# The block sums of the first MLP weight on GpSimd instead of VectorE, with new instruction orders on every engine

## The chip, the cores and the metric

The kernel runs on one core of a Trainium2 chip. The metric is the device time of one execution in microseconds; the median of a few runs is the number that counts, lower is better.

## What is computed

Four batches of 576 tokens with 512 features (8 heads of 64) go through three stages. The first is an attention with two parts that are added: a dense one on queries, keys and values pooled by 4, and a local one in which every token sees the tokens less than 4 away.

```python
out_d = sm_attn(q_d, k_d, v_d)               # q_d: mean of 4 neighbours
out_up = np.repeat(out_d, factor, axis=2)
scores = np.where(np.abs(pos[:, None] - pos[None, :]) < factor, scale * q @ k.T, -1e9)
x = out_up + softmax(scores) @ v             # heads side by side: 512 features
```

The second mixes by a two-dimensional Fourier transform, normalises and applies an MLP; the third is a gated convolution.

```python
u = x + np.real(np.fft.fft(np.fft.fft(x, axis=1), axis=2))
un = (u - mean) / np.sqrt(var + 1e-06)
x = u + np.maximum(un @ w_ch1, 0.0) @ w_ch2  # 512 -> 2048 -> 512
gate = sigmoid(conv of 5 taps along the tokens)
out = (gate * (x @ w_val)) @ w_out
```

## The kernel before

Work is cut into 12 units of 192 tokens, three to a batch. A unit runs its LayerNorm, the MLP and the gated convolution; the attention and the Fourier mixing of the next batch run in between. TensorE multiplies float16 numbers: each float32 operand is split into a high and a low half and three products of halves are added. The splitting, the softmax, the LayerNorm and all sums fall to VectorE, ScalarE and GpSimd, the loads and stores to the DMA queue of SyncE. The first unit (function `steps32`, L1276 and L1287) still multiplies in float32, since the split weights are not ready then.

**Startup.** Batch 0 has a startup of its own (`chain0`): the scores of the local attention come in three groups g0, g1, g2 (matmuls `dS`, L1608 and L1618), VectorE takes their maxima (`score_max`, L1631, tile `dmx`), ScalarE the exponentials, VectorE divides (`score_norm`), the Fourier mixing follows (`pp`, `DS`, additions into `X` at L521), then the mean of a token (`mean`, matmuls `st` at L1888) and its subtraction (`centre`, L1892, result `u`). The first matmul of the MLP (`ph<-u,W`, L1276) waits for `u`. All weights are rounded in the same time by integer steps on VectorE (L614 and L515, tiles `W`). The attention of batch 1 starts here too: its queries and keys are loaded into tiles called `X` (L524, `X<-in_k_dram`, in two halves) and its scores are `dS<-X` at L822.

**Seven products.** Units 6 to 11 compute the first MLP matmul (`seven`, L1333) with seven block products in place of eight. That needs sums and differences of blocks of the first weight. They are made once, in units 3 and 4, by eight calls of `sums_w1` (S_SUMS = 3.4 to 4.3): a call loads four blocks of 128x256 from a copy of the rounded weight in DRAM (`w1f`, written by `store_w1`, L1235, as soon as each eighth of the weight is rounded), makes four sums (L1243, tile `sx`), splits them (`so`) and stores them to DRAM (`sums`, L1248); `load_sums` brings them back for every unit (L524, `W<-sums`).

```python
for o, p, q, op in ((2, 1, 2, ALU.add), (1, 0, 1, ALU.subtract), (0, 2, 0, ALU.subtract), (3, 3, 0, ALU.subtract)):
    V.tensor_tensor(out=x[:, o], in0=x[:, p], in1=x[:, q], op=op)          # L1243
```

**Order.** What each engine does in which order is written out by hand: the table `ORDER` (L53) holds for every engine, the DMA queue among them, a list of event numbers (`118` or `118.2`, the third instruction of event 118), and at the end of the program every instruction is chained to the one before it in its list. An instruction that waits therefore holds up all that stand behind it on its engine, a store in SyncE's list holds up the loads behind it.

Of the kernel before, what the change touches and what calls it, by code (L numbers as in the profile page):

```python
# [54 lines left out]
0 2 1 3 4 11 5 13 7 6 14 8 9 15.0 16.0 10 15.4 12 16.1 15.2 15.1 15.3 195.1 201 119.2 122.1 15.5 123.1 16.2 119.0  # L55
195.0 123.0 205 185.0 119.3 119.1 122.0 204 206 170 199 172.1 203 200 171 173 172.0 174 185.2 219.1 185.1 318.0 202
237.1 219.0 237.0 238 292 317.1 316.1 293 296.0 270.0-1 296.1 270.2 297 317.0 316.0 279 332 367.1 367.0 349 318.1-2
353 378.1 368.0 378.2 368.1 378.0 369 370.0 435.1 370.1 387.1 387.0 378.4 378.3 387.2 394.1 394.0 387.3-4 394.2
397.0-1 386 488.0 394.3 397.2 394.4 398 402.0-1 488.1 402.2 397.4 397.3 435.0 436.0 437.0 418 436.1 409.1 409.0 402.3
409.2 402.4 415.1 409.4 415.0 409.3 415.2 422.0-2 415.4 415.3 475 437.1 422.4 422.3 494.1 494.0 437.2 491 462 492.0  # L60
505 492.1 493 520 530 540 503 528.1 528.0 551 528.2 562.0 544 583.1 562.1 569 583.0 548 576.1 576.0 581 563 591 598
605 613 621.1 621.0 628 635.1 635.0 611 643.1 643.0 622 651 657 665 672 679.1 641 679.0 670 680 684 703 706 707
""",
    "gpsimd": """
0.0 5 136.1 136.0 137 0.1 139 183.0 294.0 195.0-1 183.1-3 193 219.1 219.0 219.2 237.1 195.2 225.0-2 237.0 237.2 225.3
238.1 238.0 238.2 267.1 267.0 275 277 121 282.1 280.1 280.0 282.0 283.1 283.0 285.0 294.1-3 291.0-1 298.0 291.2-5
# [6 lines left out]
30.1 30.0 20 21 18 0 32.0-1 32.3 32.2 25 28 41.1 41.0 48.0 131.0 38 23 48.1 27 48.2 56 48.3 54.0 31 131.1 54.1-3 65.0  # L73
58.0 34 65.1 42 63 59 71.0-1 71.3 71.2 77.1 77.0 58.1 73 86 81.0 55 85 60 68 130 83 75 52.0 81.1 52.1-3 81.2 92 70.0
# [6 lines left out]
302.1 224.4 249.4 249.1 302.0 253.5 249.2 241 269 274 253.6 257.0 236 246 257.3 225.0 303.0 292.0 253.7 249.5 253.8
304.0 302.3 253.9 243 278 253.10-11 257.1-2 303.3 261.0 292.1 267.1 253.12-13 284 257.4-5 263.0 292.3-4 292.2 253.14
306.0 263.1 263.3 299.0 263.2 251 288 293.0 292.5 303.1 261.1 302.2 293.1 263.4 300 263.5 407.0 303.2 261.2-3 293.2
304.2 304.1 267.0 293.3 305 295.1 261.4-5 295.0 293.4-5 271.0-2 299.1 273.0 299.2-3 273.2 273.1 296.0 310 271.3 273.3
275.1 314 327 275.0 277.0-1 304.3 275.2 277.2 296.1-3 335 280.0 296.4 280.1 296.5 306.2 306.1 282 297.0 283 297.1
297.3 309 299.4 407.1 306.3 261.6 297.4 285.0-2 323 297.5 297.2 407.2 285.3 286 291.0-1 342 291.2 338 326.0 291.3
294.0 291.4 326.1 294.1-2 350.0 322 313.0 350.1 291.5 339 326.2 311.0 291.6 326.3 298.2 298.1 354 311.1 333.1 357 364
313.1 328.3 328.2 333.0 329.3 298.0 328.1 332 331.3 328.0 334.3 329.1 329.0 329.2 331.0-1 407.4 319 331.2 334.0 334.2
334.1 371 341 347.0 344.0 379 344.1 333.2 355.0 347.1 345.1 462.1 324 345.0 347.2 366 333.3 347.3-5 355.1-2 356.1 388
347.6 355.3 356.2 407.3 347.7-9 356.0 359.0-1 345.2-3 361.0-1 395 400 347.10 359.2 356.3 378.0 376.3 378.1-2 406.0  # L90
# [387 lines left out]
def attn_moe_kernel(ctx, tc, q_t, k_t, v_p, v_w, w1, w2, w_val, conv_t, w_out, c_feat, c_seq, c_band, c_eye, c_plm, out):  # L478
# [23 lines left out]
    V, A, G, T = nc.vector, nc.scalar, nc.gpsimd, nc.tensor  # L502
# [734 lines left out]
    def sums_w1(i, kc):  # L1237
# [4 lines left out]
        for o, p, q, op in ((2, 1, 2, ALU.add), (1, 0, 1, ALU.subtract), (0, 2, 0, ALU.subtract), (3, 3, 0, ALU.subtract)):  # L1242
            V.tensor_tensor(out=x[:, o], in0=x[:, p], in1=x[:, q], op=op)  # L1243
# [871 lines left out]
```

## Time and profile before

| what | us |
|---|---|
| runs | 656.77, 656.94, 660.54; median 656.94 |
| profiled execution | 658.47 |
| span in its trace | 656.7 |
| TensorE busy | 643.9 (98%) |
| VectorE busy | 526.3 (80%) |
| ScalarE busy | 353.9 (54%) |
| GpSimd busy | 105.6 (16%) |

The trace covers the span from the first instruction to the last; 1.8 us of the profiled execution lie around it. Engines are called PE (TensorE), PEld (its weight loads), DVE (VectorE), ACT (ScalarE), POOL (GpSimd) and SPq (the DMA queue of SyncE). A granted clock of 1.00 is TensorE's upper level of 2.4 GHz, 0.50 the lower of 1.2 GHz. "[1.67 <-DMA X]" at the end of a row means that the engine stood idle for 1.67 us before it and that the DMA of X ended the wait.

### The profile page before, as it was taken

The numbers are of one execution on the slowest core, as the hardware profiler recorded it, in microseconds if no ns is written. First come the engines' busy times: TensorE is split into PE (matmuls) and PEld (weight loads), VectorE is DVE, ScalarE is ACT, GpSimd is POOL, SyncE is SP. The second block draws the span as 40 slices with busy tenths as digits, with TensorE's granted clock in tenths as the row PEclk, the third lists the DMA queues.
The fourth block names the chain that finished last, engine by engine and source line by source line (L and its number), as shares of the span: only waits on it lengthen the run. The fifth ranks groups of instructions, "written<-read, shape, count | busy, mean of one in ns | idle before, by whom it ended". The sixth has DMA issues, their size and how long they took to land.

```text
span 656.7 us, 20454 instructions
## 1 busy us (share of the span) xinstructions
PE 643.9 (98%) x8646; PEld 576.8 (88%) x8647; DVE 526.3 (80%) x1148; ACT 353.9 (54%) x1051; POOL 105.6 (16%) x162
## 2 busy tenths in 40 slices
PE   9999899999999999999999999999999999999997
PEld 4777799999998887998988898997899989998995
DVE  3999799889898868779989958996878768686644
ACT  2886558788445656687453788644232333324222
POOL 0000131310121713510310163032100200200000
PEclk9969899999999999999999999999999999999999
DMA  9949485104442012334273372253445134232401
GB/s 318 411 167 312 165 320 172 60 2 141 145 140 91 1 36 75 103 119 145 75 249 115 103 259 84 84 183 118 133 135 170 66 130 138 90 130 87 157 2 49
DMA packets 44303, 89.99 MB, mean 137 GB/s; under 512 B 3391, under 2 KB 24895, under 8 KB 43186
## 3 DMA queue, kind: packets, MB, share of 16 engines
q1 hardware_dynamic: 44210, 88.67, 39.8%
q8 instruction: 68, 1.11, 0.7%
q14 instruction: 25, 0.20, 0.1%
HBM read 73.77 MB, written 16.65 MB: 138 GB/s over the span
## 4 chain that ended last, share of the span: by engine, by line
PE 77%; DVE 5%; DMA 4%; POOL 2%; ACT 2%; SPq 1%; issue 1%; DVEq 0%; ACTq 0%; POOLq 0%
PE pc L1382 23%; PE ph L1312 11%; PE ph L1333 7%; PE val L1487 6%; PE out L1503 6%; PE p L1333 5%; PE ph L1276 3%; PE pc L1287 3%; DMA X<-in_k_dram 2%; PE ab L1063 1%; PE dS L822 1%; PE st L1147 1%; PE pp L1086 1%; DMA out_dram<-osb 1%; PE pq L1086 1%; PE po L995 1%
## 5 line engine op out<-in xcount | busy, mean ns | idle before, releaser
L1382 PE MATMUL pc<-hh,W 128*128 128x192 f16 x1232 | 169.2, 246 | 0.0
L1382 PEld LDWEIGHTS <-W 128*128 128x128 f16 x1848 | 152.7, 98 | 3.5 <-issue 1.2
L1382 PE MATMUL pc<-hl,W 128*128 128x192 f16 x616 | 130.1, 246 | 0.0
L1312 PE MATMUL ph<-u,W 128*128 128x192 f16 x960 | 93.9, 246 | 0.0
L1312 PEld LDWEIGHTS <-W 128*128 128x128 f16 x960 | 79.8, 98 | 4.6 <-issue 2.0
L1333 PEld LDWEIGHTS <-W 128*128 128x128 f16 x1632 | 78.7, 98 | 3.0 <-issue 1.2
L515 DVE SCALAR_TENSOR_TENSOR W<-X,cw,W 128x192 f32<-128x192 f32 x160 | 63.0, 430 | 4.8 <-ACT W L1450 4.5
L1333 PE MATMUL ph<-u,W 128*128 128x96 f16 x960 | 65.0, 206 | 0.5 <-ACT r L1350 0.3
L1487 PE MATMUL val<-yy,W 128*128 128x192 f16 x576 | 58.5, 246 | 1.5 <-DVE yy L515 1.5
L1345 ACT ACTIVATE hh<-r 128x384 f16<-128x384 f32 x48 | 23.8, 518 | 64.8 <-DVE r L521 53.5
L1487 PEld LDWEIGHTS <-W 128*128 128x128 f16 x576 | 47.4, 98 | 3.4 <-issue 2.1
L1333 PE MATMUL p<-u,W 128*128 128x96 f16 x672 | 48.2, 206 | 0.1
L1503 PE MATMUL out<-W,gh 128*128 128x512 f16 x144 | 46.2, 379 | 0.0
L521 DVE TENSOR_TENSOR r<-ph,r 128x384 f32<-128x384 f32 (+1 forms) x48 | 21.9, 456 | 24.8 <-PE ph L1333 20.5
L836 ACT ACTIVATE dP<-dS,dmx 128x64 f32<-128x64 f32 x120 | 36.0, 335 | 0.4
L521 DVE TENSOR_TENSOR r<-p,r 128x192 f32<-128x192 f32 (+1 forms) x72 | 28.1, 419 | 6.3 <-PE p L1333 4.3
L1316 ACT ACTIVATE hh<-ph 128x384 f16<-128x384 f32 x40 | 19.0, 484 | 22.1 <-PE ph L1312 14.7
L515 DVE SCALAR_TENSOR_TENSOR hl<-r,hh 128x384 f16<-128x384 f32 x48 | 25.7, 554 | 5.7 <-ACT hh L1345 5.2
L515 DVE SCALAR_TENSOR_TENSOR W<-W,W 128x1024 int32<-128x1024 int32 x24 | 29.7, 1248 | 0.1
L515 DVE SCALAR_TENSOR_TENSOR hl<-ph,hh 128x384 f16<-128x384 f32 x40 | 21.7, 551 | 7.2 <-ACT hh L1316 7.0
L1503 PE MATMUL out<-W,gl 128*128 128x512 f16 x72 | 27.3, 380 | 0.1
L836 ACT ACTIVATION_READ_ACCUMULATOR dP<-dS,dmx 128x1 f32 x120 | 27.4, 229 | 0.0
(306 smaller groups left out, 1423.3 us busy)
## 6 DMA issues: line engine op xcount, KB each, us to landing
W<-sums SPq DMA_DIRECT2D x32, 512.0 KB
W<-in_moe_w_ch_dram SPq DMA_DIRECT2D x12, 1024.0 KB
sm<-sums SPq DMA_DIRECT2D x16, 512.0 KB
out_dram<-osb SPq DMA_DIRECT2D x17, 256.0 KB
vw<-in_vw_dram SPq DMA_DIRECT2D x8, 512.0 KB
w1f<-W SPq DMA_DIRECT2D x8, 512.0 KB
sums<-so SPq DMA_DIRECT2D x16, 256.0 KB
v<-in_vp_dram SPq DMA_DIRECT2D x24, 144.0 KB
```

Of the source, the lines that this page charges most:

```text
L515: return eng.scalar_tensor_tensor(out=out, in0=in0, scalar=scalar, in1=in1, op0=op0, op1=op1)
L521: return eng.tensor_tensor(out=out, in0=a, in1=b, op=ALU.add)
L836: A.activation(out=s_[:, z, a], in_=pss[par][:, z, a], func=AF.Exp, scale=SCALE, bias=mx[:, par, z, a:a + 1], accum_out=su[:, par, z, a:a ...
L1276: T.matmul(out=ps[:, e], lhsT=W[AT[kc * 2 + m // 8] + 1][:, o:o + 128], rhs=u()[:, kc, :], start=(kc == 0), stop=(kc == 3))
L1287: T.matmul(out=c["ps"][m // 2][:, m % 2], lhsT=W[9 + g][:, o:o + 128], rhs=hs[g // 2][:, g % 2, e, :], start=(kk == 0 and m % 2 == 0), sto ...
L1312: T.matmul(out=ps[:, e], lhsT=w1_ap(pw, kc, 2 * g + e), rhs=uh[px][:, kc, :], start=(t == 0), stop=(t == 11))
L1316: A.activation(out=h_, in_=ps, func=AF.Relu)
L1333: T.matmul(out=out[:, e * HT:e * HT + HT], lhsT=w(pw, kc, e), rhs=b_[x](px, kc), start=(kc, pw, px) == (0, 0, 0), stop=(kc, pw, px) == (1, ...
L1345: A.activation(out=h[0], in_=x, func=AF.Relu)
L1382: T.matmul(out=ps[m // 2][:, m % 2], lhsT=w2_ap(pw, kk, m), rhs=x[px][:, e], start=(kk == 0 and (pw, px) == (0, 0) and m % 2 == 0), stop=( ...
L1487: T.matmul(out=ps[:, e], lhsT=wv_ap(pw, kc, 2 * mh + e), rhs=m_["y"][px][:, kc, :], start=(t == 0), stop=(t == 11))
L1503: T.matmul(out=ps, lhsT=(gh, gl)[px][:, kc, t * 128:(t + 1) * 128], rhs=wo_ap(pw, kc), start=(n == 0), stop=(n == 11))
```

## The change

One line of the program changes the engine of the 32 sums, and the table of orders is replaced for all five engines. It is 7 lines longer, so that a line number below 53 stays and every later one grows by 7 (L1243 becomes L1250, L524 becomes L531).

```diff
-            V.tensor_tensor(out=x[:, o], in0=x[:, p], in1=x[:, q], op=op)
+            G.tensor_tensor(out=x[:, o], in0=x[:, p], in1=x[:, q], op=op)
...
     "sync": """
-0 2 1 3 4 11 5 13 7 6 14 8 9 15.0 16.0 10 15.4 12 16.1 15.2 15.1 15.3 195.1 201 119.2 122.1 15.5 123.1 16.2 119.0
...
+0 2 1 3 4 5.1 11 13 16.0 7 5.0 6 14 8 9 12 10 15.0 15.4 15.3 15.2 15.1 16.2 16.1 195.1 203 119.3 15.5 122.0 199 123.0
```

Apart from the 32 sums each engine has the instructions that it had, in another order.

First, VectorE at the start of the program. The tiles dmx_222 are the maxima of score group g0 (dS_181 and dS_183), dmx_293 those of g1. Before:

```order
L1631 TENSOR_REDUCE dmx_293<-dS_250 128x8
L1631 TENSOR_REDUCE dmx_293<-dS_248 128x8
L1631 TENSOR_REDUCE dmx_222<-dS_181 128x4
L1631 TENSOR_REDUCE dmx_222<-dS_183 128x4
L1689 TENSOR_REDUCE qkT_136<-X_134 128x288
L1689 TENSOR_REDUCE qkT_136<-kTa_137 128x288
L537 MEMSET ones_105 128x128
L1646 TENSOR_SCALAR dsu_233<-dsu_233 128x8
L1647 RECIPROCAL dsu_233<-dsu_233 128x8
```

Now:

```order
L1638 TENSOR_REDUCE dmx_222<-dS_181 128x4
L1638 TENSOR_REDUCE dmx_222<-dS_183 128x4
L1638 TENSOR_REDUCE dmx_293<-dS_248 128x8
L1638 TENSOR_REDUCE dmx_293<-dS_250 128x8
L1696 TENSOR_REDUCE qkT_136<-X_134 128x288
L1696 TENSOR_REDUCE qkT_136<-kTa_137 128x288
L1653 TENSOR_SCALAR dsu_233<-dsu_233 128x8
L1654 RECIPROCAL dsu_233<-dsu_233 128x8
L525 TENSOR_TENSOR dP_235<-dP_235,dsu_233 128x256
```

The maxima of g0 moved ahead of those of g1, and the memset behind the first division.

Second, the DMA queue of SyncE where the keys of batch 1 are loaded. `w1f<-W_114` and `w1f<-W_115` are stores of rounded eighths of the first weight, `X<-in_k_dram` the two halves of the keys. Before, eight rows behind the store `w1f<-W_114`:

```order
L524 DMA X<-in_k_dram 128x2x582
L1235 DMA w1f<-W_115 128x1024
L524 DMA vw<-in_vw_dram 128x512
L524 DMA raw<-in_moe_w_ch_dram 128x1024
L524 DMA W_123<-in_moe_w_ch_dram 128x2x1024
L524 DMA X<-in_k_dram 128x2x582
```

Now:

```order
L531 DMA v_1223<-in_vp_dram 72x2x256
L1242 DMA w1f<-W_115 128x1024
L531 DMA raw<-in_moe_w_ch_dram 128x1024
L531 DMA W_121<-in_moe_w_ch_dram 128x2048
L531 DMA X<-in_k_dram 128x2x582
L1242 DMA w1f<-W_114 128x1024
L531 DMA X<-in_k_dram 128x2x582
L531 DMA W_122<-in_moe_w_ch_dram 128x2x1024
L531 DMA X<-in_q_dram 128x2x576 x2
L1242 DMA w1f<-W_116 128x1024
```

The first half of the keys stood behind the store of W_114 and the second behind that of W_115 too; now the first half stands behind the store of W_115, which comes first, and the second right behind the store of W_114.

Third, GpSimd in the midst of units 3 and 4, where the sums now stand (ptv and vr pool the values of a batch, sx_4222, sx_4360, sx_4426 are those of three calls; sq_4526 belongs to the LayerNorm of a unit). Before:

```order
L521 TENSOR_TENSOR ptv_3881<-v4_3877 72x256
L521 TENSOR_TENSOR vr_3856<-v4_3878 72x256
L521 TENSOR_TENSOR vr_3856<-vr_3856,ptv_3881 72x256
L521 TENSOR_TENSOR sq_4526<-sq_4526 128x384
L521 TENSOR_TENSOR sq_4526<-sq_4526 128x192
L1037 TENSOR_TENSOR fs_4590<-X_2960 128x577
L1037 TENSOR_TENSOR fs_4643<-X_2960 128x577
```

Now:

```order
L528 TENSOR_TENSOR ptv_3881<-v4_3877 72x256
L528 TENSOR_TENSOR vr_3856<-v4_3878 72x256
L528 TENSOR_TENSOR vr_3856<-vr_3856,ptv_3881 72x256
L1250 TENSOR_TENSOR sx_4222<-sx_4222 128x256 x4
L1250 TENSOR_TENSOR sx_4360<-sx_4360 128x256 x4
L1250 TENSOR_TENSOR sx_4426<-sx_4426 128x256 x3
L528 TENSOR_TENSOR sq_4526<-sq_4526 128x384
L1250 TENSOR_TENSOR sx_4426<-sx_4426 128x256
L528 TENSOR_TENSOR sq_4526<-sq_4526 128x192
L1044 TENSOR_TENSOR fs_4590<-X_2960 128x577
```

Eleven sums, 128x256 each, moved in ahead of the squares of the LayerNorm, and one between them.

## Rows read from the trace of the kernel before

**Rows 1.** The page, part 1: busy time, share of the span, instructions.
```profile
PE 643.9 (98%) x8646; PEld 576.8 (88%) x8647; DVE 526.3 (80%) x1148; ACT 353.9 (54%) x1051; POOL 105.6 (16%) x162
```

**Rows 2.** Windows of 41 us: length, busy PE, PEld, DVE, ACT, POOL, PEclk, DMA share, GB/s.
```profile
41.00:82.00 41.00, 37.14 (x428) 31.38 (x428) 37.31 (x74) 25.61 (x74) 2.98 (x14) 0.90 0.75 255
82.00:123.00 41.00, 41.00 (x422) 39.93 (x421) 38.65 (x53) 28.85 (x92) 9.92 (x13) 1.00 0.60 211
```

**Rows 3.** Waits of PE over the whole span: us in total, times, longest.
```profile
PE dS L822 <- DMA X<-in_k_dram: 1.7, 1, 1.7
PE val L1487 <- DVE yy L515: 1.5, 1, 1.5
```

**Rows 4.** Windows of 10 us, columns as in rows 2.
```profile
60.00:70.00 10.00, 10.00 (x85) 7.28 (x83) 9.61 (x20) 8.67 (x22) 0.77 (x9) 1.00 0.99 337
70.00:80.00 10.00, 8.24 (x67) 7.22 (x65) 7.49 (x13) 3.63 (x11) 2.21 (x6) 0.83 0.20 76
```

**Rows 5.** Timeline of DVE from 10 us on: start, length, instruction, idle before.
```profile
10.15 1.95 DVE L1631 TENSOR_REDUCE dmx<-dS 128x8 f32<-128x512 f32 x4 [10.15 <-PE dS L1618]
...
19.28 1.29 DVE L1631 TENSOR_REDUCE dmx<-dS 128x8 f32<-128x512 f32 x2 [0.69 <-PE dS L1618]
```

**Rows 6.** Timeline of PE from 4 and from 12 us.
```profile
8.94 1.40 PE L1618 MATMUL dS<-kTa,X 64*58 64x64 f32 x80
...
12.23 3.46 PE L1753 MATMUL po<-vw,plm 64*72 64x256 f32 x15
...
18.12 1.10 PE L1618 MATMUL dS<-kTa,X 64*58 64x64 f32 x62
```

**Rows 7.** DVE by line and shape, 10 to 12.1 us: busy, mean ns.
```profile
L1631 DVE TENSOR_REDUCE dmx<-dS 128x4 f32<-128x256 f32 x2 | 0.7, 416 | 0.0
```

**Rows 8.** Timeline of PE at the end of the startup.
```profile
69.12 0.90 PE L1888 MATMUL st<-X,ones 128*128 128x192 f32 x4
...
72.16 0.29 PE L822 MATMUL dS<-X 64*58 64x64 f32 x2 [1.67 <-DMA X<-in_k_dram]
72.37 1.36 PE L1888 MATMUL st<-X,ones 128*128 128x192 f32 x4
...
74.78 3.52 PE L1276 MATMUL ph<-u,W 128*128 128x192 f32 x16
```

**Rows 9.** Timeline of DVE at the same place.
```profile
70.45 0.81 DVE L521 TENSOR_TENSOR X<-mir,DS 128x289 f32<-128x289 f32 x2
73.77 0.95 DVE L1892 TENSOR_TENSOR u<-X,st 128x768 f32<-128x768 f32 x1 [2.51 <-PE st L1888]
```

**Rows 10.** Window of 1 us on PE: busy, PEclk, DMA share, GB/s.
```profile
73.00:74.00 1.00, 1.00 (x14) 0.50 0.06 25
```

**Rows 11.** The chain that ended last, 80 to 90 us.
```profile
83.60 2.60 PE ph L1276 x16
```

**Rows 12.** Timeline of SyncE's DMA queue, 17 to 64 us (length is the issue).
```profile
41.44 0.36 SPq L1235 DMA_DIRECT2D w1f<-W  x1
...
59.44 0.34 SPq L1235 DMA_DIRECT2D w1f<-W  x1
...
61.65 0.47 SPq L524 DMA_DIRECT2D X<-in_k_dram  x1
```

**Rows 13.** The line of the sums: ns min/median/max, first and last start.
```profile
L1243 DVE TENSOR_TENSOR sx<-sx x32: 406/424/832, 271.5 to 371.2; 128x256 f32<-128x256 f32 x32
```

**Rows 14.** POOL by line and shape: busy, mean ns, idle before.
```profile
L518 POOL TENSOR_TENSOR dP<-dP,dsu 128x256 f32<-128x256 f32 x4 | 3.3, 830 | 20.0 <-ACT osb L1521 16.4 <-DVE dsu L840 3.6
```

**Rows 15.** Timeline of SyncE's queue, 363 to 378 us.
```profile
376.54 1.64 SPq L524 DMA_DIRECT2D W<-sums  x2
```

**Rows 16.** Timeline of PE, 384 to 387 us: the first product from a sum is in this row.
```profile
385.95 0.29 PE L1333 MATMUL ph<-u,W 128*128 128x96 f16 x3
```

**Rows 17.** Timeline of POOL, 211 to 220 us: two equal products.
```profile
215.15 1.50 POOL L518 TENSOR_TENSOR r<-r,vv 128x192 f32<-128x192 f32 x1
...
218.59 0.59 POOL L518 TENSOR_TENSOR r<-r,vv 128x192 f32<-128x192 f32 x1
```

More of the change, by code (lines that the diff above doesn't have):

```diff
@@ L70 @@
+419.0 423 424 402 427.1 427.0 409 415.0-2 444.0 415.3 444.1 422 430.1 450 430.0 488.1 488.0 488.2 499.0 491.0 467
+491.1 499.1 492 491.2 499.2-3 493.1 493.0 493.2 433 546.0-1 535 539 546.2-3 545.1 545.0 550 553.1 553.0 554 559 609
 639
@@ L81 @@
[L81 to L90, printed above, removed]
@@ new lines @@
+546.13 546.11-12 570.0-2 570.5 546.14 570.6 570.3-4 546.15 594.0-1 574 594.2 590 578.0-2 578.5 578.3 578.6 578.4
+594.3-4 579.2 579.1 579.3 582.1 594.5 584.1 585.0-3 585.5 594.6 585.4 585.6 579.0 594.7-8 582.2 582.0 582.3 584.3
+584.0 584.2 593.0-1 586.1 593.2-3 593.5 594.9 586.3 586.2 586.0 594.10 593.4 593.6 634.3 594.11-15 594.17 592.0
+599.0-1 594.16 599.2-3 599.5 599.4 599.6 670.1 594.19 594.18 592.1 609.0 603 596.0 609.1 620 596.1 607.0-2 607.5 607.3
+607.6 607.4 609.2 608.1-2 608.0 615.0-2 615.5 608.3 612.2 615.6 615.3-4 612.3 612.1 612.0 609.3-6 624.0-3 624.5
@@ new lines @@
+96.7 96.10 96.16 96.11 96.14-15 96.17-18 96.20 96.19 96.21-22 96.24 96.23 96.25 96.28 96.26 96.29 96.27 96.30-31 99
+100 101.0 101.2-3 101.1 101.4-6 101.8-9 101.12 101.7 101.13 101.16-17 101.20-21 101.24-25 101.28-29 101.10-11
+101.14-15 101.18-19 101.22-23 101.26-27 101.30-31 126.0 128.2 128.0-1 128.3 111.6 111.12 111.0 111.13-14 111.1 111.7
+111.15-16 111.2-3 111.17 111.4-5 111.8-11 115.24 115.0-1 115.12 115.25-26 115.2-6 115.27 115.7-10 115.28 115.11
+115.13-15 115.29-30 115.16 115.31-32 115.17 115.33 115.18 115.34-35 115.19-23 120.0 120.12-16 120.6 120.1-3 120.17
@@ new lines @@
+571.1 571.8 571.2 571.9-10 571.3-5 571.11-12 571.18 571.13-14 571.19-20 571.15-17 571.21-23 578.0-11 572.0 572.6
+572.1-2 572.7-8 572.3-4 572.9 572.5 572.12-14 572.10-11 572.15 572.18-19 572.16 572.20-23 572.17 573.0-4 573.6 573.5
+573.12 573.7 573.13 573.8-10 573.14 573.11 573.15-23 594.0 578.48 578.12 578.72 578.13-16 578.49-51 578.73 578.17
+578.52 578.18 578.74 578.19-29 578.53-57 578.30-37 578.75 578.38-47 578.58-65 578.76 578.66-68 592.0-5 578.69
+578.77-78 578.70-71 578.79-83 592.6-21 585.0-6 585.48 585.7 585.24-25 585.8-11 585.49 580.6 580.0-3 580.7-9 580.4-5
@@ new lines @@
+627.2 627.8 627.3 629.49 629.12-15 629.50 629.28-29 629.16-19 629.51-53 629.30-31 629.54-57 629.72 629.58-59 629.73
+629.20 629.60 629.21-22 629.32-33 629.23 629.34 629.61-65 629.35 629.74-75 629.66-69 629.76-78 629.36 629.70-71
+623.0-1 629.37-47 629.79-80 627.4-5 627.12 627.9-10 627.13-15 629.81-83 627.11 627.18-20 627.16 627.21-23 627.17
+623.2-19 630.0 630.6 630.1-2 637.0-1 626.22-23 637.2-3 623.20-23 630.7-8 630.3 630.9-11 630.4-5 630.18-20 630.12-13
+630.21-22 630.14-16 630.23 630.17 637.4-6 637.24 637.7 637.25-26 637.8-11 631.0 631.6-8 631.1-2 631.9-10 631.3-5
@@ new lines @@
+631.12-15 631.11 631.16-23 639.0 637.12 637.27 637.72 637.48 637.13-14 637.49-50 637.15 637.28 637.73 637.29 637.16-17
+637.30-41 637.18 637.42-47 637.51-53 637.74 637.54-59 637.75-76 637.60 637.77-80 637.61-63 637.19 637.64 637.20-21
+637.81-83 637.22-23 637.65-71 632.0-1 632.6 632.2 632.7 632.3-5 632.8-10 632.12 632.11 632.18-22 632.13 632.23
+632.14-17 641.0-8 645.0-2 645.24 645.3-4 645.25 645.5 645.26 645.6-10 645.27-28 645.11 641.9-11 645.12 645.72
+645.13-15 639.1 645.16 645.73 645.48 645.29-32 645.49 645.33-34 645.74 645.50 645.35-38 645.51 645.39 645.17-18
@@ new lines @@
+653.51-53 653.20 653.25 653.21 653.26-33 653.54 653.34-35 653.55-56 653.36 653.57 653.37-38 653.58 653.39-40 653.74-75
+653.59 653.22-23 653.60-61 653.41-43 653.62-63 653.76-79 653.64-65 653.44-47 653.66-68 653.80 652.12-17 653.69-70
+653.81-83 653.71 649.11 649.0 649.18-20 649.1 649.21-22 649.2-5 649.12-15 658.24 658.0-2 658.25 652.18 649.16-17
+649.23 654.0-1 654.6 654.2-3 658.3-5 658.26 658.6-9 658.72 658.10 658.48 658.11 658.73-74 654.4 654.7-11 654.5
+654.12-13 654.18 654.14 654.19 654.15 654.20-23 654.16-17 655.19-23 652.19-23 658.75 658.12 658.49 658.27 658.13
@@ L357 @@
+688.0 688.12 688.1-7 688.13 688.8-11 688.14-23 703 701 704 705 707.0 706.0-6 707.1-6 706.7-11 707.7-11
 """,
```

540 lines of the change are left out of this document (261 added, 279 removed), and 8 rows, old and new, of the table ORDER.

## The prediction

> **What bounds the kernel now.** I read the page first. TensorE is busy for 643.9 us of a span of 656.7, VectorE for 526.3 and GpSimd for 105.6 [rows 1]: TensorE sets the time, and what can be won are the 12.8 us in which it is idle and the stretches in which it runs at its lower clock. The windows of 41 us say where these lie. Between 41 and 82 TensorE is busy for 37.14 of 41 us at a mean clock of 0.90, and from 82 to 123 for all of its 41 us at 1.00 [rows 2]. So the loss is in the startup and next to nothing in the stretch behind it. The list of TensorE's waits names the largest single one: scores of batch 1 that wait 1.7 us for a DMA of keys; next comes one of 1.5 us for VectorE in `val` [rows 3]. In the last startup window before the loss VectorE is busy for 9.61 of 10 us, and in the next, from 70 to 80, for 7.49 [rows 4]: up to about 71 us VectorE has no holes to speak of and paces the start, and behind that TensorE does. The timeline of VectorE shows where it does wait: its first instruction comes at 10.15, when the scores are there, and at 19.28 it waits 0.69 for the scores of group g2 [rows 5].
>
> **The sums themselves.** 32 instructions of 0.424 (the median) leave VectorE: 13.6 us between 271.5 and 371.2 [rows 13]. They join GpSimd. The trace shows no sum of this shape there; the nearest row is a product of the same shape, 128x256 with two operands, at 830 ns mean [rows 14], so I take 32 x 0.83 = 26.6 us, on an engine that is busy 16% of the span. TensorE, busy 98% of the span [rows 1], is the bound there, so the 13.6 us come off an engine that is not, and I count them at 0. They could be worth at most what small waits there are; the cost on the other side is the second rival's.
>
> **The start of VectorE.** Before, the four maxima wait for the scores of g1, start at 10.15 and take 1.95 [rows 5]. Now the two maxima of g0 come first, and TensorE's order has the last nine products of g0 ahead of the 32 of g1, where before g1's stood first. The 40 products take from 8.94 to 10.34, 0.035 each [rows 6]; nine are done at 8.94 + 0.32 = 9.26, and with the delay of rows 5 (32 products end at 10.06, VectorE starts at 10.15, so 0.09) the maxima of g0 (2 x 0.416, 0.7 overlapped [rows 7]) run from 9.35 to 10.05. Those of g1 cannot begin before 10.34 + 0.09 = 10.43 and need 1.95 - 0.7 = 1.25, so they end at 11.7 where before the four ended at 12.1: 0.4 us won. It must pass the wait at 19.28, which is for TensorE: from 12.23 to 19.22 TensorE works without a hole towards the scores of g2 [rows 6]. In the new order one product `po` less stands ahead of them, two of the instructions that take 3.46 / 15 = 0.23 each [rows 6], so that end moves by 0.46 too. I take 0.4 us for the start; the bounds are 0 (TensorE holds VectorE at 19.28 as before) and 0.7 + 0.4 = 1.1 (the wait goes altogether).
>
> **VectorE's work up to the mean.** TensorE's last products ahead of the MLP, the second pair of `st`, need the last addition into `X`, which ended at 70.45 + 0.45 = 70.9 [rows 9]. I compared what VectorE does ahead of that addition in the two orders: it is the same list but for a few short integer steps. I count 0, with 0.2 either way. The addition then ends at 70.5.
>
> **The keys.** Before, the second half of the keys was issued at 61.65, after the store that waited until 59.44 for a rounding step of VectorE [rows 12], and landed when TensorE went on at 72.16, 1.67 us late; only then came the second pair of `st` at 72.37 [rows 8], 1.47 after the addition at 70.9. In the new order the first half waits for the store of W_115 and the second for that of W_114, which before was freed at 41.44 [rows 12]. Both loads are then issued about 42. Even if they take as long as before, 72.1 - 61.65 = 10.4 us, they are there at 52.5, some 18 us early. With the keys in place, the scores fill TensorE while the addition runs, and the second pair of `st` follows it by the 0.06 us with which such steps follow each other. That takes 1.47 - 0.06 = 1.4 us. Behind it comes the subtraction `u` (0.95 us at 73.77 [rows 9]), which the next product `ph` waits for, with its length unchanged.
>
> **The clock.** After the wait the granted clock is 0.50, the lower level, from 73 to 74 [rows 10], and back at 1.00 by 77. Four `st` took 1.36 there and 0.90 before the wait; the first 16 `ph` 3.52 [rows 8], and 2.60 at full clock [rows 11]. If TensorE doesn't idle there, the lower level doesn't come, and 0.46 + 0.92 = 1.4 us go. What is left of idle time is short: `u` is waited for, but scores of batch 1 can fill that now. The bounds are 0 and 1.4; I take 1.4, since the fall came right behind this wait.
>
> **What comes next.** The chain behind `u` is bound by TensorE (41.00 of 41 us busy [rows 2]), so an earlier start moves all of it, and the wait of 1.5 in `val` [rows 3] moves along, since VectorE's and GpSimd's work ahead of it stays in the order that made it late. Sum: 0.4 + 0 + 1.4 + 1.4 = 3.2 us. The profiled execution took 658.47 us (span 656.7 and 1.8 around it) and would take 655.3; it lies 1.5 above the median of the runs shown, 656.94, and the predicted median is 656.94 - 3.2 = 653.7.
>
> **Rivals.**
> - *Nothing is kept.* VectorE paces the startup, and a new order of some 1000 instructions can put a wait of a microsecond anywhere in it; or VectorE reaches the addition at 70.9 as before because TensorE held it at 19.28, and then TensorE stands idle for `st` instead of the keys, with the same fall of the clock. For it speaks that VectorE is busy for 9.61 of 10 us up to 70 [rows 4]; against it that TensorE waited 1.67 us for the keys and not for VectorE. Keeping at most 0.7 gives 656.2 to 656.9.
> - *Slower: the sums come late.* The two last stores of sums and the loads of unit 6 stand one behind the other in SyncE's list; the loads were issued at 376.54 [rows 15] and the first product from them began at 385.95 [rows 16]. The two are 512 KB each, which at the 255 GB/s of the startup window [rows 2] is an estimate of 4.1 us, so 385.95 - 376.54 - 4.1 = 5.3 are spare. Each of eight rounds takes 4 x (0.83 - 0.42) = 1.6 us more on GpSimd, 13 in all if each round hangs on the one before. It decides from the point at which these loads are issued later than 376.54 + 5.3 = 381.8. Then TensorE waits 13 - 5.3 = 7.7 us and pays the 1.4 of the lower clock again; with the startup's 3.2 taken off that is 656.94 + 7.7 + 1.4 - 3.2 = 662.8, and 666.0 with nothing won there. Against it speaks that before a round came only about every 12 us (32 sums in 100 us [rows 13]) and GpSimd has a share of 16%, so a round can stretch by 1.6 without touching the next.
> - *VectorE and GpSimd block each other.* In the trace of before one of the 32 sums on VectorE took 832 where the median is 424 [rows 13], and of two equal products on GpSimd one took 1.50 and one 0.59 [rows 17]: instructions of the two do stretch each other. With 32 more on GpSimd and 0.41 lost in each, 13 us of VectorE's work would be given back, all that it was freed of. VectorE isn't the bound there, so TensorE would see 1 to 2 us at most: 654.7 to 655.7. That is the forecast plus this. The Trainium skill (SBUF — State Buffer, Who interferes with whom) has this as a rule: GpSimd's only pair of ports is the second pair of VectorE, and a VectorE instruction with two inputs in SBUF contends with a GpSimd instruction that reads SBUF, one blocking the other fully. Its page Perfetto Trace Analysis (Optimizing Scalar/DVE Operations) adds that "offloading operations between those two might not help". By that rule the sum would be 13 us of freed VectorE time less 13 lost, which leaves the 0 that I took, and the row of 832 agrees with it.
> - *More is won.* The new orders also take away the wait in `val` and the other small ones, up to 2 us with the bound of the start: 651.
>
> That the change does not do what it says is excluded: the 32 sums stand in GpSimd's list, and the keys stand ahead.
>
> **How the numbers follow.** The forecast, 653.7, has a chance of 0.58, with a range of its own from 652.3 (start at its bound of 1.1, other orders 0.7) to 655.3 (no gain by the clock, 0.2 of VectorE's work more). Nothing kept has 0.18, the sums late 0.06, the blocking 0.12, more won 0.06. The range of 0.8 reaches from 651.0 to 657.5: it leaves out the late sums and the ends of the others. About 1% (6.6 us) is what a measurement of this kernel can tell from no change. Faster by more than that means below 650.4, which would need most of "more won" beyond its price: 0.04. Slower means above 663.5, the late sums alone or an order that went wrong: 0.05. That leaves 0.91 for within 1%.
>
> **What would show it.** Right: no wait for `X<-in_k_dram` in the list of TensorE's waits, both halves issued near 42; the first maxima near 9.4; `u` begun some 2.3 us earlier than 73.77 (0.4, 1.4 and the 0.46 of `st`); the first 16 `ph` at 2.60 with a clock of 1.00; TensorE's busy time down by some 1.4; the sums at about 0.83 on GpSimd, the loads of sums landed before 384. Wrong: a wait of `st` or `ph` for VectorE that takes the place of the keys, a lower clock at 73 all the same, or a wait of L1340 (before L1333) for sums near 386.

## The result, and the profile after

The changed kernel takes 662.48 us (median of 10 runs, 660.75 to 663.69), the kernel before 656.96 beside it (10 runs): the ratio is 1.0075, with a 95% interval of 1.0055 to 1.0095. 653.7 was predicted. Its profiled execution took 662.02 us with a span of 660.1. Two of the twelve executions of run e2 below took 1307.5 us, a slow state that no other run had and that nothing here explains; they are left out. The line numbers of the changed kernel are those of before plus 7.

The page, part 1, of the changed kernel:

```profile
PE 645.8 (98%) x8647; PEld 577.3 (87%) x8647; DVE 528.6 (80%) x1116; ACT 354.0 (54%) x1051; POOL 128.2 (19%) x194
```

VectorE gave 32 instructions of 13.6 us away and is busy for no less than before (528.6 for 526.3 [rows 1], and for 528.2 in a second profile of the kernel before, run b0); GpSimd took 22.6 us more (128.2 for 105.6). The waits of TensorE over the span, the largest first (us in total, times, longest):

```profile
PE ph L1319 <- ACT u L1199: 1.2, 1, 1.2
...
PE dPT L862 <- issue: 0.8, 1, 0.8
PE p L1340 <- ACT dP L843: 0.7, 1, 0.7
PE dO L879 <- ACT PT L865: 0.7, 2, 0.5
PE st L1154 <- DVE sq L528: 0.6, 1, 0.6
...
PE st L1154 <- POOL sq L528: 0.5, 1, 0.5
```

The wait for the keys [rows 3] is gone, and so is that of 1.5 in `val`, which came back as 1.2 in `ph` (L1319). New are many short ones, for ScalarE, VectorE and GpSimd. The windows of 41 us place them. Before (length, busy PE, PEld, DVE, ACT, POOL, PEclk, DMA share, GB/s):

```profile
246.00:287.00 41.00, 41.00 (x597) 36.55 (x595) 31.85 (x66) 27.66 (x95) 16.89 (x20) 1.00 0.36 114
287.00:328.00 41.00, 40.91 (x484) 36.94 (x482) 37.25 (x95) 26.14 (x73) 4.88 (x5) 1.00 0.31 93
328.00:369.00 41.00, 40.73 (x535) 35.87 (x536) 36.86 (x82) 20.14 (x58) 4.18 (x10) 1.00 0.55 172
369.00:410.00 41.00, 40.68 (x683) 34.98 (x682) 30.51 (x76) 35.49 (x135) 18.60 (x23) 1.00 0.46 152
```

After:

```profile
246.00:287.00 41.00, 40.11 (x581) 35.17 (x579) 30.52 (x61) 26.86 (x90) 20.58 (x25) 1.00 0.31 94
287.00:328.00 41.00, 39.42 (x453) 34.52 (x451) 35.37 (x81) 24.37 (x73) 14.25 (x15) 1.00 0.35 105
328.00:369.00 41.00, 39.91 (x470) 35.30 (x471) 38.73 (x72) 19.66 (x50) 12.93 (x22) 1.00 0.43 137
369.00:410.00 41.00, 39.21 (x703) 33.30 (x694) 27.87 (x61) 33.51 (x131) 21.28 (x27) 1.00 0.50 160
```

TensorE was idle for 0.7 us of these 164 before and is for 5.4 after: this is units 3 to 6, the stretch in which the sums are made, and in the prediction it has no term. In the startup the keys and the clock went as forecast, and VectorE's start did not. VectorE's start after:

```profile
9.91 0.76 DVE L1638 TENSOR_REDUCE dmx<-dS 128x4 f32<-128x256 f32 x2 [9.91 <-PE dS L1625]
...
19.30 1.29 DVE L1638 TENSOR_REDUCE dmx<-dS 128x8 f32<-128x512 f32 x2 [0.74 <-PE dS L1625]
```

TensorE at the end of the startup, after:

```profile
71.39 0.92 PE L1895 MATMUL st<-X,ones 128*128 128x192 f32 x4
...
73.35 2.87 PE L1283 MATMUL ph<-u,W 128*128 128x192 f32 x16 [0.52 <-DVE u L1899]
```

SyncE's queue, after:

```profile
40.85 0.38 SPq L531 DMA_DIRECT2D X<-in_k_dram  x1
...
41.78 0.47 SPq L531 DMA_DIRECT2D X<-in_k_dram  x1
```

Both halves of the keys are issued near 42 (before 61.65 for the second [rows 12]), `st` follows at 71.39 in 0.92 and the first `ph` begins at 73.35 where it was 74.78 [rows 8]. The windows of 1 us give a granted clock of 1.00 throughout from 70 to 80. The sums on GpSimd, at the line that was L1243 [rows 13] (ns min/median/max, first and last start):

```profile
L1250 POOL TENSOR_TENSOR sx<-sx x32: 722/727/1320, 269.2 to 373.0; 128x256 f32<-128x256 f32 x32
```

### The profile page after: what moved, and what is told of

Read it like the earlier page. It is cut to its first block, busy times and chain, and to the rows that moved or that the text cites. A ratio compares the mean times of both kernels' runs of the same rounds, so it can differ in the third digit from the quotient of the medians.

```text
span 660.1 us, 20462 instructions
## 1 busy us (share of the span) xinstructions
PE 645.8 (98%) x8647; PEld 577.3 (87%) x8647; DVE 528.6 (80%) x1116; ACT 354.0 (54%) x1051; POOL 128.2 (19%) x194
## 4 chain that ended last, share of the span: by engine, by line
PE 53%; DVE 8%; ACT 3%; issue 1%; DMA 1%; POOL 0%; SPq 0%; DVEq 0%; ACTq 0%; POOLq 0%
PE pc L1389 18%; PE ph L1340 7%; PE out L1510 6%; PE val L1494 6%; PE p L1340 5%; PE ph L1319 4%; DVE W L522 2%; ACT dP L843 1%; DMA kT<-in_k_dram 1%; PE ab L1070 1%; DVE uc L525 1%; PE st L1154 1%; PE dO L879 1%; PE dS L829 1%; PE po L1002 1%
## 5 line engine op out<-in xcount | busy, mean ns | idle before, releaser
L1319 PE MATMUL ph<-u,W 128*128 128x192 f16 x960 | 94.9, 246 | 1.2 <-ACT u L1199 1.2
L1319 PEld LDWEIGHTS <-W 128*128 128x128 f16 x960 | 80.0, 98 | 4.1 <-issue 2.8
L1340 PEld LDWEIGHTS <-W 128*128 128x128 f16 x1632 | 79.5, 98 | 3.1 <-issue 1.0
L522 DVE SCALAR_TENSOR_TENSOR W<-X,cw,W 128x192 f32<-128x192 f32 x160 | 69.2, 472 | 0.6 <-ACT W L1457 0.2
L1340 PE MATMUL ph<-u,W 128*128 128x96 f16 x960 | 66.3, 206 | 0.2 <-DVE r L528 0.2
L1340 PE MATMUL p<-u,W 128*128 128x96 f16 x672 | 49.1, 206 | 0.7 <-ACT dP L843 0.7
L1250 POOL TENSOR_TENSOR sx<-sx 128x256 f32<-128x256 f32 x32 | 25.4, 795 | 33.9 <-DMA sx<-w1f 25.8
L528 POOL TENSOR_TENSOR uc<-X 128x384 f32<-128x384 f32 x6 | 7.0, 1168 | 109.1 <-DVE u L1200 109.0
```

Source lines behind the costliest of these rows:

```text
L522: return eng.scalar_tensor_tensor(out=out, in0=in0, scalar=scalar, in1=in1, op0=op0, op1=op1)
L528: return eng.tensor_tensor(out=out, in0=a, in1=b, op=ALU.add)
L1250: G.tensor_tensor(out=x[:, o], in0=x[:, p], in1=x[:, q], op=op)
L1319: T.matmul(out=ps[:, e], lhsT=w1_ap(pw, kc, 2 * g + e), rhs=uh[px][:, kc, :], start=(t == 0), stop=(t == 11))
L1340: T.matmul(out=out[:, e * HT:e * HT + HT], lhsT=w(pw, kc, e), rhs=b_[x](px, kc), start=(kc, pw, px) == (0, 0, 0), stop=(kc, pw, px) == (1, ...
```

## The experiments

Two theories. C: the sums on GpSimd hold VectorE up, and TensorE waits behind it. O: the new orders put work that TensorE waits for late in units 3 to 6, whichever engine adds. The first four runs cross them.

**e1_sums_back.** The changed kernel with the sums back on VectorE, its orders kept:

```diff
-            G.tensor_tensor(out=x[:, o], in0=x[:, p], in1=x[:, q], op=op)
+            V.tensor_tensor(out=x[:, o], in0=x[:, p], in1=x[:, q], op=op)
```

> The changed kernel with the 32 sums back on VectorE, each put into VectorE's list where it ran on GpSimd by the changed kernel's trace; all other orders as changed. Theory C (the sums on GpSimd block VectorE: 43 of its instructions that overlap a sum were 8.6 us longer than before, and TensorE waits behind them in units 3 to 6): the loss goes and the start's gain of about 2 us stays, 655 to 658. Theory O (the new orders put needed work late in units 3 to 6, whatever engine adds): VectorE gets 5 us more to do, 661 to 664.

660.83 (9 runs) beside 657.31 for the kernel before (32 runs); ratio 1.005 (1.0029 to 1.0072). Neither forecast is met, O's by 0.2: of the loss of 5.5 us two thirds (3.5) stay with no sum on GpSimd.

**e2_sums_alone.** The opposite: the kernel before, only the sums moved.

```diff
-            V.tensor_tensor(out=x[:, o], in0=x[:, p], in1=x[:, q], op=op)
+            G.tensor_tensor(out=x[:, o], in0=x[:, p], in1=x[:, q], op=op)
```

> The kernel before with only the 32 sums moved to GpSimd, each put into GpSimd's list where it ran on VectorE by the trace of before; no other order changed. Theory C: 659 to 662, new waits of TensorE between 270 and 400. Theory O: 656 to 658, as before.

657.97 (10 runs), ratio 1.0016 (0.9994 to 1.0038): 0.7 us more in the median and 1.0 by the ratio, which this interval doesn't tell from none.

**e3_no_sums.** The changed kernel without the sums on any engine.

```diff
-        for o, p, q, op in ((2, 1, 2, ALU.add), (1, 0, 1, ALU.subtract), (0, 2, 0, ALU.subtract), (3, 3, 0, ALU.subtract)):
-            G.tensor_tensor(out=x[:, o], in0=x[:, p], in1=x[:, q], op=op)
```

> The changed kernel with the 32 sums left out (the loaded blocks are split and stored as they are), so that no engine does them; orders as changed. Theory C: 655 to 657. Theory O: 660 to 662.

659.01 (12 runs), ratio 1.0024 (1.001 to 1.0038): still above the kernel before, although it has less to do, and between the forecasts of the two theories. By e1, O is the larger part of the loss; the sums add to it on either engine.

**e4_keys_alone.** The kernel before with the one load of the prediction's largest terms moved (SyncE's list):

```diff
 L524 DMA X<-in_k_dram 128x2x582
+L524 DMA X<-in_k_dram 128x2x582
 L1235 DMA w1f<-W_115 128x1024
 L524 DMA vw<-in_vw_dram 128x512
 L524 DMA raw<-in_moe_w_ch_dram 128x1024
 L524 DMA W_123<-in_moe_w_ch_dram 128x2x1024
-L524 DMA X<-in_k_dram 128x2x582
```

> The kernel before with one load moved: the second half of the keys of batch 1 right behind the first half in SyncE's list, ahead of the store of W_115. By the prediction's steps on the keys and the clock: 1.4 + 1.4 us less, 654.2, with ph 2.3 us earlier and a granted clock of 1.00 at 73. Rival (VectorE sets the end of the startup anyway and the clock falls on other short waits): 656 to 657.

656.82 (12 runs, 655.91 to 658.44), ratio 0.9993 (0.9975 to 1.0011). In the trace the prediction's steps come out: `ph` at 72.90, 1.88 earlier, a clock of 1.00, a span of 654.2 for the 656.7 of before. The median is lower by only 0.5, which this interval doesn't tell from none. So the question was whether the execution that had been profiled stands for the kernel.

**b0_before_again.** The kernel before once more, no edit:

> The kernel before once more, unchanged, for a second profile of it. If the wait of 1.67 us for the keys and the lower clock behind it belong to the one execution that was profiled first (its time was 1.5 above the median), this profile has neither, a span of about 654 to 655, and ph at about 73.5 in place of 74.78. If they belong to the kernel: wait and clock as before.

655.79 and a span of 654.0. TensorE's timeline of this execution:

```profile
70.78 0.29 PE L822 MATMUL dS<-X 64*58 64x64 f32 x2 [0.43 <-DMA X<-in_k_dram]
71.00 0.92 PE L1888 MATMUL st<-X,ones 128*128 128x192 f32 x4
...
72.96 2.87 PE L1276 MATMUL ph<-u,W 128*128 128x192 f32 x16 [0.41 <-DVE u L1892]
```

Its window of 1 us at 73, as in [rows 10]:

```profile
73.00:74.00 1.00, 1.00 (x6) 1.00 0.02 8
```

The keys were late by 0.43 in place of 1.67, the clock stayed at the upper level, the second pair of `st` took 0.92 and not 1.36. In the five other profiles with this order of the loads the wait was 1.39 (t1), 0.89 (s3), 0.13 (s1), 0.06 (e2) and none (t5); the clock fell to 0.50 behind the 1.39, as behind the 1.67, and stayed at 1.00 in the others. The keys land 9.1 to 10.4 us after their issue in the four that waited longest, about when they are needed: one execution waits, another does not. The mean of the seven waits is 0.65.

That gives a way to read the traces without this chance. All of them wait once near 220 us, and what follows can be compared by the time from the end of that wait to the end of the span. With the startup of before the row is `val<-yy` (L1487) after its wait of 1.5; with the changed startup it is `ph<-u` (L1312 before, L1319 in the changed kernel) after its wait of 1.2. Up to that row TensorE has started 2519 to 2521 matmuls in every one of these traces, so it stands at the same point of the work. The last column, rest, is the span less the start of the row.

| run | row starts | span | rest |
|---|---|---|---|
| before, first profile | 222.30 | 656.7 | 434.4 |
| before, second profile (b0) | 219.85 | 654.0 | 434.2 |
| e4, keys alone | 219.77 | 654.2 | 434.4 |
| e2, sums alone | 220.66 | 656.2 | 435.5 |
| changed kernel | 220.22 | 660.1 | 439.9 |
| e1, sums back | 219.66 | 658.2 | 438.5 |
| e3, no sums | 221.62 | 658.7 | 437.1 |

The three traces with the orders of before agree within 0.2. Against b0's 434.2 the changed kernel loses 5.7 behind 220 us; its orders lose 2.9 without any sum and 4.3 with the sums on VectorE. Not all of the 5.7 is waiting: behind the row TensorE is idle for 9.0 us in the changed kernel and for 5.4 in b0, and busy for 430.9 and 428.8, with the same number of matmuls. Some 2 us are thus TensorE's own busy time; no run tells whether its own new order makes it so.

**s1_new_245_405, s2_old_245_405, s3_new_245_345.** The orders of two kernels joined at a moment: up to it each engine has its list from the one, behind it what is left in the order of the other. s1 has the lists of before up to 245 us, the changed ones from 245 to 405, and those of before again; s2 is its reverse, changed, before from 245 to 405, changed; s3 is s1 with 345 in place of 405. The sums are on VectorE in all three. One place of VectorE's list, s3 against the kernel before:

```diff
-L518 TENSOR_TENSOR uc<-uc,r_3520 128x768
-L515 SCALAR_TENSOR_TENSOR W_123<-X,cw,W_123 128x192 x3
 L839 TENSOR_SCALAR dsu<-dsu 128x16
 L840 RECIPROCAL dsu<-dsu 128x16
...
+L518 TENSOR_TENSOR uc<-uc,r_3520 128x768
+L1193 TENSOR_TENSOR u<-uc,u 128x768
```

> The kernel before (sums on VectorE), with the changed orders of all engines only for what ran between 245 and 405 us; ahead of and behind that the orders of before. If the new orders of units 3 to 6 are what costs (the waits of TensorE at 267, 317, 322, 328, 383, 388 and 393 us that run e1 shows with the sums on VectorE, 4.1 us together): 660 to 661.5. Rival, that the loss comes from the new start or from the end: 656.5 to 658.

> The reverse of s1: the changed orders (sums on VectorE) everywhere but for what ran between 245 and 405 us, where the orders of before stand. If the new orders of that stretch are what costs: 656 to 657.5, and no wait of TensorE over 0.3 us between 245 and 405. Rival: 660.

> As s1, but the changed orders only between 245 and 345 us. The waits at 267, 317, 322 and 328 of run e1 are 2.5 us: 659 to 660 if these count in full; the rest of s1's loss belongs to 345 to 405, where ScalarE does 16 exponentials in a row. If only the later stretch costs: 657 to 658.

Beside 657.68 for the kernel before (21 runs) s1 took 663.05 (6 runs; ratio 1.0083, 1.006 to 1.0106), s2 656.03 (12 runs; 0.9977, 0.9961 to 0.9992) and s3 661.39 (10 runs; 1.0055, 1.0032 to 1.0077). The whole loss comes and goes with the orders of this stretch, and more than half with those of 245 to 345. s2 met its forecast; s1 and s3 took 1.5 and 1.4 more than the upper ends of theirs. TensorE's waits from 245 to 405 us in s1:

```profile
PE ab L1063 <- ACT FH L1046: 0.9, 1, 0.9
PE dPT L855 <- issue: 0.8, 1, 0.8
PE p L1333 <- ACT dP L836: 0.7, 1, 0.7
PE dO L872 <- ACT PT L858: 0.7, 2, 0.5
PE ab L1063 <- DVE p2b L568: 0.4, 1, 0.4
```

The same in s2:

```profile
PE dS L812 <- ACT dP L836: 0.9, 1, 0.9
PE ab L1063 <- DVE AL L515: 0.2, 1, 0.2
```

The waits of e1 stand in s1 again, in another startup and another end; the orders of before have none of them (the 0.9 for `dP` in s2 is at 246, where the two lists are joined). Behind the row near 220 s1 has 440.0 left (659.8 - 219.79), s3 438.6 (660.2 - 221.62) and s2 434.2 (654.3 - 220.07), as the kernel before. s1 has 1.5 more left than e1 with the same waits, so a part of its loss may come of the joining; s2, in which the loss is gone, doesn't hang on that.

How one of them comes about is seen in s3, on three engines at the wait of `dPT` (0.79 at 269). VectorE:

```profile
265.19 3.38 DVE L518 TENSOR_TENSOR uc<-uc,r 128x768 f32<-128x768 f32 x1
```

GpSimd:

```profile
265.03 0.72 POOL L521 TENSOR_TENSOR vr<-vr,ptv 72x256 f32<-72x256 f32 x1
265.72 2.04 POOL L518 TENSOR_TENSOR dP<-dP,dsu 128x512 f32<-128x512 f32 x2
```

ScalarE:

```profile
268.61 0.84 ACT L1192 ACTIVATE u<-uc 128x768 f16<-128x768 f32 x1 [3.33 <-DVE uc L518]
269.36 0.99 ACT L878 ACTIVATE X<-dO 128x464 f32<-128x464 f32 x2
```

The product `uc` of a LayerNorm has 0.96 us of work (in the kernel before, at 261.95). Here it begins 0.16 after an instruction of GpSimd and ends at 268.57, 0.8 after the last of the three that GpSimd does without a gap (267.76): it stood for 2.4 us. ScalarE has `u` ahead of the eviction `X<-dO` in its list, and `u` waits for `uc`. That TensorE then waits for the evicted PSUM is inferred, since the profile names no releaser for `dPT`; the next run tests it. None of this has to do with the sums, which aren't running then; it is the order of three lists.

**t1_two_moves.** Run s3 with two instructions of VectorE moved.

```diff
+L518 TENSOR_TENSOR uc<-uc,r_3520 128x768
 L839 TENSOR_SCALAR dsu<-dsu 128x16
 L840 RECIPROCAL dsu<-dsu 128x16
-L518 TENSOR_TENSOR uc<-uc,r_3520 128x768
...
-L883 TENSOR_REDUCE qkT<-X 128x288
 L1156 TENSOR_TENSOR uc<-X,st 128x768
...
 L515 SCALAR_TENSOR_TENSOR FL<-fF,s_x_4148,FH 128x2x289 x2
+L883 TENSOR_REDUCE qkT<-X 128x288
```

> Run s3 (the changed orders only between 245 and 345 us, sums on VectorE, 661.4) with two instructions of VectorE moved: the product uc<-uc,r (at 265.19 in s3, 3.39 long) ahead of dsu, so that it runs before GpSimd's three products begin, and the reduction qkT<-X (1.35 at 312.57) from ahead of the Fourier steps fs, fF, FL to behind them, where the orders of before have it. Theory: uc stood blocked by GpSimd for 2.4 us and takes about 1 now, TensorE's wait of 0.79 at 269 goes; the Fourier steps begin 1.3 earlier and the waits at 319.5 (0.87) and 324.4 (0.43) go: 2 us less, 659.3. Rival (the stretch is slow as a whole and these places only show it): the waits come up elsewhere, 661.

660.05 (12 runs) beside 657.49 (29 runs); ratio 1.0044 (1.002 to 1.0068). `uc` on VectorE and the waits of TensorE in the stretch:

```profile
264.38 0.95 DVE L518 TENSOR_TENSOR uc<-uc,r 128x768 f32<-128x768 f32 x1
```

```profile
PE ab L1063 <- DVE p2b L568: 1.6, 1, 1.6
PE pq L1086 <- ACT DS L1113: 0.5, 1, 0.5
```

`uc` takes 0.95, and the waits of `dPT` and of `ab` for FH (0.8 and 0.9) are gone. The block itself only moved: `u<-uc,u` of the same LayerNorm now runs beside GpSimd's three instructions and takes 2.95 at 266.59 (0.96 in s3), again until 0.8 after the last of them (269.54 and 268.72), but the eviction no longer stands behind it. The second wait of `ab`, for VectorE's p2b, grew from 0.4 to 1.6, as the reduction now stands in front of it. The rest behind the row near 220 falls from 438.6 in s3 to 436.9 (659.1 - 222.16): TensorE is idle there for 0.8 us less in net and busy for 0.9 less. In the times the gain is not clear, as the intervals of s3 and t1 overlap; the median lies between the two forecasts.

**t5_qkT_later.** The reduction moved behind that chain too.

```diff
 L515 SCALAR_TENSOR_TENSOR FL<-fF,s_x_4148,FH 128x2x289 x2
-L883 TENSOR_REDUCE qkT<-X 128x288
...
 L1193 TENSOR_TENSOR u<-uc,u 128x768
+L883 TENSOR_REDUCE qkT<-X 128x288
```

> Run t1 with the reduction qkT<-X set still later on VectorE, behind u<-uc of the same LayerNorm (at 331.9 in s3). In t1 it stood in front of the chain of r, AL and uc and TensorE's wait for AL and p2b at 328.9 grew from 0.45 to 1.62. Theory (in this stretch VectorE's list is one chain and whatever of 1.3 us is put in ahead of a step that TensorE waits for costs that): the wait at 328.9 falls to 0.4 again and the time to 658.8. Rival: it comes up behind, 660.

659.57 (12 runs) beside 657.67 (17 runs); ratio 1.0037 (1.0016 to 1.0057). The wait for p2b is 0.4 again, and another has come up behind it:

```profile
PE ph L1312 <- DVE iv_y L570: 1.1, 1, 1.1
```

The rest is 437.0 (657.2 - 220.19), no better than t1: here the rival was right. As these runs suggest, VectorE's list from 300 to 335 us is one chain of the Fourier steps and the LayerNorm that TensorE follows closely, and one misplaced reduction is only handed on along it.

**t3_best_sums_gps, t4_sums_twice_gps, s2_again.** The price of the engine in the best orders found: s2 with the sums on GpSimd, and with each done twice there (so the sums are others).

```diff
-            V.tensor_tensor(out=x[:, o], in0=x[:, p], in1=x[:, q], op=op)
+            G.tensor_tensor(out=x[:, o], in0=x[:, p], in1=x[:, q], op=op)
...
+            for _ in range(2):
+                G.tensor_tensor(out=x[:, o], in0=x[:, p], in1=x[:, q], op=op)
```

> Run s2 (the changed orders but those of 245 to 405 us, 656.0 with the sums on VectorE) with only the 32 sums moved to GpSimd, where they ran on VectorE: the price of the engine alone, with orders that have little waiting in that stretch. Theory C (VectorE stands blocked for a GpSimd sum, some 0.27 us per sum, and TensorE waits behind it now and then): 657 to 658. If the engine costs nothing: 656; if its 13.6 us freed on VectorE help: 655.

> Run t3 with each sum done twice on GpSimd (the second over the result of the first, so the sums differ): 64 instructions, 25 us more on GpSimd, none on VectorE. Theory C: VectorE's other instructions grow by another 5 to 9 us and the time by as much again as t3 lost against s2 or more, 658 to 661. If GpSimd's work costs nothing: as t3.

> Run s2 once more beside t3 and t4 on the same chip: 656.0 expected, a ratio to before of 0.996 to 0.999.

On one chip, beside 657.49 for the kernel before: s2 656.01 (12 runs; 0.9988, 0.9969 to 1.0006), t3 657.07 (12 runs; 0.9994, 0.9975 to 1.0014), t4 677.21 (5 runs; 1.0296, 1.0261 to 1.033). The three pairs that differ only in the engine give 1.1 (t3 to s2), 0.7 (e2 to before) and 1.6 us (changed kernel 662.48 to e1 660.83), always the same way; only for e2 is there an interval of the pair itself, and it doesn't exclude none. Behind the row near 220 the same pairs differ by 2.2 (t3 436.2, s2 run again 434.0), 1.3 and 1.4. Instruction by instruction, 43 of VectorE's that overlap a sum in t3 are 8.9 us longer than in s2 run again. In t4 VectorE's instructions grow by another 5.4, within the forecast. But the second dose costs 20 us, far over it, and so most of it not by this. ScalarE's waits in t4 from 245 to 425 us:

```profile
ACT so L1246 <- POOL sx L1244: 17.1, 5, 8.4
```

TensorE's longest in t4:

```profile
PE st L1147 <- DVE uc L521: 4.6, 1, 4.6
```

The split `so` stands in ScalarE's list and waits there for the sums, 17.1 us in all (6.3 in t3, 2.7 in the changed kernel), with the exponentials, Fourier halves and evictions behind it. So sums can come too late, and a doubling does it, but by another path than the prediction's rival: through ScalarE's list, while no product of unit 6 waits for a sum in t4. How much of the 20 us goes this way is not measured.

The best version is s2: the changed orders in the startup and the end, those of before from 245 to 405, sums on VectorE. It is 6.4 us faster than the changed kernel (656.03 for 662.48); against the kernel before it gains 0.1 to 0.2%, with one interval just below 1 and one across it.

## Why the prediction was wrong

*What comes next, and the sum.* This is the step that failed. The prediction said that an earlier start moves all that follows, since TensorE bounds it and the work "stays in the order that made it late". It read the new orders where they touch the startup, and GpSimd's list for the sums, and gave all other moves no term. The rest behind 220 us grew by 5.7, of which 4.3 come with the orders alone (e1), and it is 434.2 again with the orders of before from 245 to 405 us (s2). TensorE's busy time, which was to fall by 1.4, rose by 1.9 (645.8 for 643.9). That TensorE is busy for 98% does not mean that the others have slack at every place: in the stretch of the loss VectorE was busy 37.25 of the 41 us from 287 before, and a step that TensorE follows closely can't move by a microsecond there. "Nothing is kept" named such a wait, but only in the startup and at a price of no more than what was to be won; no rival had a price for a loss by orders alone, and only the chance of 0.05 for "slower" names "an order that went wrong".

*The keys and the clock.* The mechanism was right: both loads near 42, no wait, the clock at 1.00, `st` at its full speed. The clock's term was too large: the first 16 `ph` take 2.87 at that clock and not the 2.60 of a later group, so 0.65 went and not 0.92, and `u` began 1.4 us earlier (72.34), not 2.3. What failed besides is the base. The terms, 1.4 and 1.4, were taken from a profiled execution that was 1.5 us over the median, and were then taken off the median. The second profile of the same kernel has 0.43 of that wait and nothing of the clock, and e4, which has the load moved alone, gains 0.5 us in the median, within its interval. At the row near 220 the changed kernel is 2.1 us ahead of the first profile (220.22 for 222.30) and 0.4 behind the second (219.85). The sum should have asked whether the 1.5 us between the two were this very wait.

*The start of VectorE.* 0.4 was taken, with 0 as a bound; 0 held. The maxima of g0 began at 9.91, not at 9.35, as TensorE's products of this row began at 9.39 and not at 8.94, and those of g1 ended no earlier; the wait for g2 at 19.30 stayed (0.74 for 0.69). TensorE held VectorE there. VectorE's addition ended at 71.08 + 0.45 = 71.5, where 70.5 was forecast; TensorE had other work up to `st` at 71.39 and did not idle for it.

*The sums themselves.* 25.4 us on GpSimd (32 of 0.795 in the mean) for 26.6 forecast. The median sum takes 0.727; of the four products of the row that was taken, with a mean of 0.83, one took 1.49 and the others 0.61.

*VectorE and GpSimd block each other* (0.12). This rival was right in its mechanism and nearly in its size: 43 VectorE instructions that overlap a sum in the changed kernel are 8.6 us longer than their twins before (0.27 a sum, where 0.41 was taken). Of the 13.6 us freed, VectorE's busy time keeps 2.9 (531.5 in e1, 528.6 in the changed kernel), 2.7 from s2 run again to t3, and 4.9 or 6.8 from the two profiles of before to e2, and the kernel pays 0.7 to 1.6 where 1 to 2 was written. A row shows it, VectorE at three steps of the convolution, which take 1.07 together when alone (at 356.49):

```profile
358.80 2.14 DVE L522 SCALAR_TENSOR_TENSOR W<-X,cw,W 128x192 f32<-128x192 f32 x3
```

GpSimd meanwhile:

```profile
359.19 2.33 POOL L1250 TENSOR_TENSOR sx<-sx 128x256 f32<-128x256 f32 x3 [8.08 <-DMA sx<-w1f]
```

And TensorE behind it:

```profile
362.48 0.56 PE L1154 MATMUL st<-sq,ones 128*128 128x192 f32 x2 [0.65 <-DVE sq L528]
```

This wait of `st` is there in e2 and t3 too (0.4 each, with 0.4 and 0.6 more for `uc` of the same LayerNorm), and in no trace with the sums on VectorE. The rule of the Trainium skill (SBUF — State Buffer, Who interferes with whom), that the port pair which these two engines share is an exclusive lock, agrees with `uc` in s3 and `u` in t1, which each stood until GpSimd's three instructions were done. The Trainium skill's warning that moving work between these two engines might not help (Perfetto Trace Analysis, Optimizing Scalar/DVE Operations) agrees with t3 against s2, where it cost 1.1.

There is a second way, which the prediction did not have: a sum in GpSimd's list holds up GpSimd's own work behind it. In the changed kernel one stands between the two squares of a LayerNorm:

```profile
314.20 0.99 POOL L528 TENSOR_TENSOR sq<-sq 128x384 f32<-128x384 f32 x1 [3.30 <-ACT sq L1165]
315.16 1.25 POOL L1250 TENSOR_TENSOR sx<-sx 128x256 f32<-128x256 f32 x1
316.36 1.10 POOL L528 TENSOR_TENSOR sq<-sq 128x192 f32<-128x192 f32 x1
```

TensorE's `st` behind the second square waits for it; this is the 0.5 of `st` for `POOL sq` in the list of waits above.

*The sums come late* (0.06). The loads of sums were issued at 380.33, 3.8 later than before, and the products that use them at about 390, 4.4 later. They came in time, as no product L1340 waits for a load of sums.

What stays open: which moves of the stretch from 345 to 405 cost the last 1.4 us of s1 over s3, why e3, without sums, still loses 2.9, and why TensorE's busy time grew; no run undid the moves one by one, and none changed TensorE's order alone.

## What to carry to other kernels

A change that also replaces a table of orders is two changes: run each alone before either is priced. A term read from one profiled execution may be that execution's own; where its time stands off the median by as much as the term, take a second profile first. Work moved from VectorE to GpSimd gives back much of what it frees, and where the lists are fixed by hand the engine that looks idle is waited for at fixed places.

## What the runs showed of the hardware that was not expected

GpSimd can keep VectorE out for longer than one instruction: twice, three of its instructions in a row held a VectorE product until the last had ended (`uc` in s3, 3.38 us for 0.96, and `u` in t1, 2.95 for 0.96). Of VectorE's instructions in the changed kernel that overlap GpSimd for at least 30% and did not overlap it before, the TENSOR_TENSOR (18) are longer than before by 0.34 us in the mean, the SCALAR_TENSOR_TENSOR (62) by 0.17, the TENSOR_SCALAR (12) by 0.19 and up to 0.74, the TENSOR_REDUCE (14) by 0.00: these reductions passed untouched. The landing of one load, 9.1 or 10.4 us after its issue, decided some 2.4 us of a 657 us kernel (222.30 and 219.85 in the table), through a wait of 1.67 and the lower clock (0.50) that followed it, while after a wait of 0.43 at the same place the clock stayed at 1.00.
